# Reordering the first projections of an attention and GLU kernel, with half sums of the exponentials on GpSimd

## The chip, the cores and the metric

The kernel runs on one core of one Trainium2 chip. The metric is the time of one execution in device microseconds; the median of three runs of the kernel before is 205.53 us.

## The reference, cut to what matters

x has 2048 rows of 448; there are 16 heads of 28. `_layernorm` has no weights. The first block is an attention whose feature maps are softmaxes over the 28 elements of a head:

```python
h  = x  + _A_ref(_layernorm(x), wqkv, w_phi, wo)
h2 = h  + _B_ref(_layernorm(h), w_gate, w_up, w_down)

def _A_ref(x, wqkv, w_phi, wo):
    q, k, v = x @ wqkv, split into 16 heads of 28
    pq, pk = q @ w_phi, k @ w_phi                       # per head
    phi_q = concat(softmax(pq), softmax(-pq))
    phi_k = concat(softmax(pk), softmax(-pk))
    kv  = einsum("bhsf,bhsd->bhfd", phi_k, v);  z = sum over s of phi_k
    num = phi_q @ kv;  den = phi_q . z + 1e-6
    return (num / den) @ wo

def _B_ref(x, w_gate, w_up, w_down):
    return (sigmoid(x @ w_gate) * (x @ w_up)) @ w_down
```

## The kernel before

The 2048 rows are 16 tiles of 128. Products contract 64 rows at a time: two matmuls with 64 input rows each run side by side in the upper and lower half of the array, so a product over 448 inputs is written as two operations, an `a` with 8 matmuls and a `b` with 6; `b` adds to banks that `a` has just written with the other half of the array, and so waits until `a` has drained.

Every operation has a name, and every engine works off its names in an order that is written out by hand in the table `ORDER`, one string for each of `sp` (SyncE, which issues nearly all DMAs), `act` (ScalarE), `pe` (TensorE), `dve` (VectorE) and `pool` (GpSimd). A graph of reads and writes adds the semaphore waits; an operation may stand in the string of either of two engines (a copy out of PSUM on ScalarE or VectorE, for instance), and it runs on the engine in whose string its name stands. Nothing is reordered while the kernel runs: an operation that waits holds up all that follows on its engine.

The names that matter, with the number of a tile (0 to 15) behind most of them:

- `x0` to `x14`: loads of the input (x0 and x1 of one tile, the others of two). `ld_k`, `ld_v`, `ld_q`: the key, value and query weights; `ld_q` are four transposing DMAs into `WqT`. `ld_wo`, `ld_wg`, `ld_wu`, `ld_wd`: the weights of the output projection and of the GLU.
- `wT`, `wTe`: the key weights transposed on TensorE and copied out. `wsp`, `wex`: `w_phi` spread into a block diagonal matrix (with `hmask`). `w2m0_0` to `w2m0_3` and `w2e0_0` to `w2e0_3`: the key weights folded with `w_phi` into `Wk`, by a product and a cast out of PSUM; `w2m1` and `w2e1` the same for the query weights (`Wq`). `w2m1_k` reads all four `WqT`, and the four share two banks, so `w2m1_3` and `w2m1_2` need the casts of `w2m1_1` and `w2m1_0`.
- `bst`, `agg`: mean and variance of a tile (VectorE). `pow1`: the scale, to the power -1/2 (GpSimd), for tiles 0, 1, 2, 3 singly, for 4 and 5, 6 and 7, then for 8 to 11 and for 12 to 15 in one instruction; `nm1` the negated mean. `xn`: the normalized tile. `xT`: its transpose, for tiles 0 to 3 on TensorE (`xT0e` to `xT3e` copy it out), from tile 4 on by a transposing DMA on SyncE's queue (4 to 15).
- `ppa`, `ppb` (tiles 0 and 1, then 2 and 3): the projected keys, into banks 0 and 1. `vva`, `vvb`: the values of the same tiles, into banks 2 and 3. From tile 4 on `pva`, `pvb` make keys and values of one tile side by side. `v1`: the values copied out. `ek`: exp and exp of the negated keys (ScalarE, two instructions), in a ring of five buffers.
- `ss`: the sums of the exponentials over each head, a reduction of 896 elements of bf16 into 32 (VectorE, L675); `rs`: their reciprocals; `phi`: the exponentials times those (L685; VectorE or GpSimd); `kva`, `kvb`: the product with the values, summed over all tiles in banks 6 and 7; `seed`: the small constant there. `kvzA` to `kvzD`: the masked copies out of them.
- `pqa`, `pqb`, `eq`: projected queries of 512 rows and their exponentials. `qs`, `num`, `rsm`, `qq`, `b`, `c`, `rden`, `o`: numerator, denominator and quotient of a tile; `oT`: its transpose (tiles 0 and 1 on TensorE with `oT0e`, `oT1e`; later ones by DMA). `woa`, `wob`: the output projection of two tiles; `bs2`, `h`, `hn`, `hT`: the residual, its normalization and transpose. `ga`, `gb`, `sig`, `hh`, `dn`, `dp`, `dm`, `fin`, `out`: the GLU.
- `warm`: matmuls of zeros. `wwo`, `wgu`: no instruction, only waits of TensorE for the weights of the later stages.

Banks of PSUM are shared: the joint products of an even tile reuse banks 0 and 2, of an odd tile 1 and 3, so `pva` of a tile waits for the `ek` and `v1` of two tiles before. Of the order before, the part of TensorE up to tile 5:

```python
"... w2m0_3 xT1 xT0 warm7 warm8 warm9 xT3 ppa0 ppb0 xT2 vva0 seed vvb0 ppa2 ppb2 vva2 vvb2 kva0 "
"w2m1_1 w2m1_0 kvb0 pva4 kva1 pvb4 pva5 w2m1_3 w2m1_2 pvb5 ..."
```

Of the kernel before, what the change touches and what calls it, by code (L numbers as in the profile page):

```python
# [6 lines left out]
ALU = mybir.AluOpType  # L7
ACT = mybir.ActivationFunctionType
AX = mybir.AxisListType
# [9 lines left out]
class Graph:  # L19
# [90 lines left out]
    def emit(self, nc):  # L110
# [86 lines left out]
D = 448  # L197
H = 16
DH = 28
# [82 lines left out]
    ),  # L282
    "pool": (
# [44 lines left out]
def build(nc, A_x, A_wqkv, A_w_phi, A_wo, B_w_gate, B_w_up, B_w_down, out):  # L328
    S = A_x.shape[1]
    assert A_x.shape[0] == 1 and A_x.shape[2] == D and S == 2048  # L330
    NT = S // P
    NCH = S // 512
    x_t = A_x[0].rearrange("(p n) d -> p n d", p=P)
    out_t = out[0].rearrange("(p n) d -> p n d", p=P)
    wd_v = B_w_down.rearrange("(ft p) n -> p ft n", p=P)
    NV2 = 4
    NX, NO, NH, NPHI, NS, NE, NV, NSG, NHH = 3, 4, 3, 3, 4, 5, 5, 4, 2

    with ExitStack() as es:
        def sb(name, shape, d=dt.bfloat16):  # L340
            return es.enter_context(nc.sbuf_tensor(name, shape, d))
        f32 = dt.float32
        ident = sb("ident", [P, P])
# [676 lines left out]
```

## Time and profile before

| | us |
|---|---|
| median of three runs | 205.53 (205.25 to 205.82) |
| span of the profiled execution, first to last instruction | 202.0 |
| the two apart | 3.5 |
| TensorE busy | 196.1 |
| VectorE busy | 132.2 |
| ScalarE busy | 92.7 |
| GpSimd busy | 56.4 |

The page gives of the profiled execution its span alone, 202.0 us; the 3.5 us between it and the median of the runs lie before the first and after the last instruction. The granted clock of TensorE is 1.00 in every stretch named here. In the profile a row of the timeline is start, duration, engine, line, operation, what it writes and reads with sizes, and how many instructions were merged; the brackets at its end tell how long the engine had been idle and who ended that. PE is TensorE, PEld its loads of weights, DVE VectorE, ACT ScalarE, POOL GpSimd, SPq the queue of SyncE.

### The profile page before, as it was taken

To read this page: it belongs to the slowest core of one execution; us is meant where nothing else is said; L and a number is where in the kernel's file an instruction comes from. 1 tells how busy PE (TensorE), PEld (TensorE's weight loads), DVE (VectorE), ACT (ScalarE), POOL (GpSimd) and SP (SyncE) were. 2 spreads that over 40 slices of the span, in tenths; PEclk is the share of its full clock that TensorE was granted. 3 is DMA by queue.
4 is the path that set the end of the run, shared out by engine and by line. 5 is a ranking of instruction groups with operands and counts; after the bars stand their busy time and mean duration, and the time that the engine had idled before them with its cause. 6 is when DMAs were issued, how large, how long until landed. Compare 5 with 4: busy or idle time off the path is not lost.

```text
span 202.0 us, 5885 instructions
## 1 busy us (share of the span) xinstructions
PE 196.1 (97%) x2516; PEld 113.1 (56%) x2516; DVE 132.2 (65%) x319; ACT 92.7 (46%) x191; POOL 56.4 (28%) x95
## 2 busy tenths in 40 slices
PE   7899999999989999999999999999999999999995
PEld 4735656565558778676444444555555555554443
DVE  4899999978899677767758977436432422272224
ACT  3768998899772636222333342324422212222220
POOL 6579949533433613600041010001400000000000
PEclk9999999999999999999999999999999999999999
DMA  6955345849963320251005311030312000004003
GB/s 170 281 117 158 68 83 78 237 154 285 292 181 86 65 43 3 52 81 29 0 3 123 81 26 26 5 73 28 71 33 52 0 3 0 0 3 136 0 0 94
DMA packets 32491, 16.27 MB, mean 81 GB/s; under 512 B 24720, under 2 KB 31568, under 8 KB 32464
## 3 DMA queue, kind: packets, MB, share of 16 engines
q1 hardware_dynamic: 32336, 15.86, 32.0%
q8 instruction: 20, 0.33, 0.7%
q14 instruction: 7, 0.06, 0.1%
q10 hardware_dynamic: 128, 0.03, 0.1%
HBM read 8.34 MB, written 1.84 MB: 50 GB/s over the span
## 4 chain that ended last, share of the span: by engine, by line
PE 91%; DVE 4%; DMA 2%; SPq 1%; issue 1%; POOL 1%
PE psum L311 84%; PE psum L941 5%; DMA x_sb<-in_A_x_dram 2%; SPq L415 1%; DVE st L545 1%; PE psum L538 1%; DVE st L829 1%; POOL rst L833 1%; PE psum L612 0%; DVE hn_pad L851 0%; DVE xnT L531 0%; DVE b_sb L801 0%; DVE Wk L531 0%; DVE c_sb L804 0%; DVE rsm L798 0%
## 5 line engine op out<-in xcount | busy, mean ns | idle before, releaser
L311 PE MATMUL psum<-xnT,wg_sb 64*128 64x512 bf16 (+1 forms) x490 | 93.1, 333 | 0.2
L311 PE MATMUL psum<-xnT,wu_sb 64*128 64x512 bf16 (+1 forms) x490 | 92.9, 333 | 0.0
L913 ACT ACTIVATE sg_sb<-psum 128x512 bf16<-128x512 f32 (+1 forms) x70 | 34.8, 511 | 91.3 <-PE psum L311 90.8
L914 DVE SCALAR_TENSOR_TENSOR hhT<-sg_sb,psum 128x512 bf16<-128x512 bf16 (+1 forms) x70 | 38.9, 576 | 54.4 <-ACT sg_sb L913 54.2
L311 PEld LDWEIGHTS psum<-xnT,wg_sb 64*128 64x128 bf16 x490 | 44.4, 94 | 22.5 <-DVE hhT L914 4.2
L311 PEld LDWEIGHTS psum<-xnT,wu_sb 64*128 64x128 bf16 x490 | 44.4, 94 | 13.1
L311 PE MATMUL psum<-wd_sb,hhT 64*128 64x448 bf16 x336 | 36.9, 349 | 0.0
L311 PEld LDWEIGHTS psum<-wd_sb,hhT 64*128 64x128 bf16 x336 | 17.6, 94 | 14.5 <-DVE x_sb L836 0.5
L311 PE MATMUL psum<-Wk,xnT 64*128 64x448 bf16 x112 | 22.1, 350 | 0.2
L311 PE MATMUL psum<-wv_sb,xnT 64*128 64x448 bf16 x112 | 22.2, 351 | 0.1
L845 POOL TENSOR_SCALAR ve<-ssq 128x1 f32<-128x1 f32 x11 | 2.2, 200 | 55.0 <-ACT junk L842 54.8
L675 DVE TENSOR_REDUCE ss<-hhT 128x32 f32<-128x896 bf16 x16 | 16.6, 1054 | 0.3 <-ACT hhT L672 0.2
L721 ACT ACTIVATE eq<-psum 120x1024 bf16<-120x1024 f32 x16 | 15.7, 1024 | 1.0 <-PE psum L311 0.8
L685 POOL TENSOR_TENSOR phi<-hhT,rs 128x896 bf16<-128x896 bf16 x8 | 13.6, 1711 | 6.2 <-DVE rs L681 3.8
L311 PE MATMUL psum<-xnT,Wq 64*120 64x512 bf16 x112 | 15.0, 384 | 0.1
L810 POOL TENSOR_TENSOR o_pad<-c_sb,rden 128x448 bf16<-128x448 bf16 x10 | 9.3, 935 | 14.9 <-DVE rden L806 14.8
L311 PE MATMUL psum<-wo_o,oT 64*128 64x448 bf16 x56 | 13.2, 349 | 0.0
L311 PE MATMUL psum<-wo_e,oT 64*128 64x448 bf16 x56 | 13.1, 349 | 0.0
L941 PE MATMUL psum<-wd_sb,hhT 128*128 128x448 bf16 (+2 forms) x70 | 11.1, 315 | 0.0
L948 DVE SCALAR_TENSOR_TENSOR x_sb<-psum,x_sb 128x448 bf16<-128x448 f32 (+2 forms) x17 | 9.4, 592 | 2.7 <-PE psum L941 1.6
L311 PEld LDWEIGHTS psum<-Wk,xnT 64*128 64x128 bf16 x112 | 7.7, 94 | 5.6 <-PE psum L311 1.0
L801 DVE TENSOR_TENSOR b_sb<-psum,qq 128x464 bf16<-128x464 f32 x16 | 10.2, 637 | 0.7 <-PE psum L311 0.5
(103 smaller groups left out, 234.0 us busy)
## 6 DMA issues: line engine op xcount, KB each, us to landing
out_dram<-x_sb SPq DMA_DIRECT2D x15, 112.0 KB, 1.8
x_sb<-in_A_x_dram SPq DMA_DIRECT2D x7, 224.0 KB, 4.0
wd_sb<-in_B_w_down_dram SPq DMA_DIRECT2D x7, 224.0 KB, 4.0
wg_sb<-in_B_w_gate_dram SPq DMA_DIRECT2D x3, 448.0 KB, 6.3
wu_sb<-in_B_w_up_dram SPq DMA_DIRECT2D x3, 448.0 KB, 6.7
wv_sb<-in_A_wqkv_dram SPq DMA_DIRECT2D x2, 224.0 KB, 3.9
wk_sb<-in_A_wqkv_dram SPq DMA_DIRECT2D x2, 196.0 KB, 3.5
wo_e<-in_A_wo_dram SPq DMA_DIRECT2D x1, 336.0 KB, 3.1
```

The lines of the kernel that those rows point to most:

```text
L311: p = e.matmul(o, lhsT=w, rhs=r, start=st, stop=sp, tile_position=(row, 0))
L415: return op(eng, name, lambda e: e.dma_start(dst, src), r=r, w=w, dma="in" if eng == "sp" else "ain", nring=48 if eng == "sp" else 8, kb=kb)
L675: op("dve", "ss%d" % t, lambda e: e.tensor_reduce(ss[:, s, :].rearrange("p (b h) -> p b h", h=2), eks.rearrange("p b (d h) -> p b h d", h= ...
L685: return e.tensor_tensor(phi[:, sp, :, :, :].rearrange("p b a n -> p (b a) n")[:, :, 0:56].rearrange("p b (d h) -> p b d h", h=2), eks.rea ...
L721: op("act", "eq%d_%d%s" % (c, i, "pm"[sg]), lambda e, sg=sg: e.activation(eq[c][:, sg, 2 * i:2 * i + 2, :].rearrange("p g n -> p (g n)"), ...
L801: op("dve", "b%d" % t, lambda e: e.tensor_tensor(h3(b_sb), OMv[:, :, :, 0:EV], h2(qq)[:, :, :, None].to_broadcast([P, NB, 8, EV]), ALU.mul ...
L810: return e.tensor_tensor(o_pad[:, t % NO, off:off + D].rearrange("p (h d) -> p h d", h=H), c_sb[:, t % NS, :, 0:DH], rden[:, t % NS, :][:, ...
L845: op(("pool", "dve"), "ve%d" % t, lambda e: e.tensor_scalar(ve2[:, t:t + 1], ssq2[:, t:t + 1], 1.0 / D ** 3, EPS, op0=ALU.mult, op1=ALU.ad ...
L913: op("act", "sig" + nm, lambda e: e.activation(sg_sb[:, k, 0:N], bk(bg)[:, 0:N], ACT.Tanh, scale=0.5), r=[B(bg)], w=[("sg", k)])
L914: op("dve", "hh" + nm, lambda e: e.scalar_tensor_tensor(out=hhT[(t0 // 4) % NHH][:, ff, ns], in0=sg_sb[:, k, 0:N], scalar=1.0, in1=bk(bu)[ ...
L941: p = e.matmul(bk(b)[:, lo:hi], lhsT=hb[:, ff, TS(t)], rhs=wd_sb[:, ff, lo:hi], start=ff == 0, stop=ff == FT - 1)
L948: op("dve", "fin%d%s" % (t, nm), lambda e: e.scalar_tensor_tensor(out=h_sb[:, t, lo:hi], in0=bk(b)[:, lo:hi], scalar=0.5, in1=h_sb[:, t, l ...
```

## The change

It has three parts. The two loads of the value weights move in SyncE's queue from places 7 and 12 to places 6 and 7, right behind x2, and with that x4, x8 and x6 move back; `vva0` stands first of TensorE's products, ahead of `ppa0`. For six key tiles (3, 5, 7, 9, 11, 13) GpSimd adds the two halves of each group of 56 exponentials into a float32 buffer of 448 elements (`hs`, four buffers, in the space of `hhT0`, which the GLU uses later), and `ss` of such a tile reduces these. And the orders of all five engines are written anew up to the middle of the attention: the normalization of tile 0 stands ahead of the statistics of tiles 2 and 3; all four `w2m1` come before `pva4`; of the `phi`, four run on GpSimd instead of eight; `kvzA` goes to VectorE and `kvzD` to ScalarE; `o1` to VectorE, `oT1e` to ScalarE; `rden6` stands behind `h3` and `h2`, and `nm2` ahead of `o6`; `wwo` and `wgu` stand later; two `warm` are gone. From `ga0_10` on the order of TensorE is as it was.

```diff
     "sp": (
-        "x1 x0 ld_k0 ld_k2 x2 x4 ld_v2 x8 x6 ld_q2 ld_q1 ld_v0 x10 ld_q0 ld_q3 xT4 x12 x14 xT5 xT6 xT7 xT8 xT9 xT10 "
+        "x1 x0 ld_k0 ld_k2 x2 ld_v2 ld_v0 x4 x8 x6 ld_q2 ld_q1 x10 ld_q0 ld_q3 xT4 x12 x14 xT5 xT6 xT7 xT8 xT9 xT10 "
...
     "act": (
-        "wphi kvzones nm1_1 wTe0 wTe2 wTe3 w2e0_0 nm1_3 w2e0_2 w2e0_1 xT0e xT3e ek0 ek1 v1_0 nm1_6 v1_1 ek3 ek2 v1_2 "
-        "v1_3 w2e1_1 nm1_8 w2e1_0 ek4 v1_4 w2e1_2 ek5 v1_5 w2e1_3 v1_6 ek6 nm1_12 v1_7 ek7 ek8 v1_8 eq0_0p ek9 v1_9 "
...
+        "wphi wTe0 wTe2 wTe3 w2e0_2 w2e0_0 w2e0_3 nm1_3 nm1_4 ek0 ek1 v1_1 v1_0 w2e1_1 ek2 w2e1_0 v1_2 ek3 v1_3 "
+        "w2e1_2 ek4 v1_4 nm1_8 ek5 v1_5 w2e1_3 v1_6 ek6 par ek7 v1_7 ek8 v1_8 ek9 v1_9 ek10 kvzones v1_10 ek11 v1_11 "
...
     "pe": (
-        "warm0 warm1 warm2 wsp warm3 wT0 wT1 warm4 wT2 wT3 warm5 w2m0_0 w2m0_1 w2m0_2 warm6 w2m0_3 xT1 xT0 warm7 "
-        "warm8 warm9 xT3 ppa0 ppb0 xT2 vva0 seed vvb0 ppa2 ppb2 vva2 vvb2 kva0 w2m1_1 w2m1_0 kvb0 pva4 kva1 pvb4 pva5 "
-        "w2m1_3 w2m1_2 pvb5 pva6 kvb1 kva2 pvb6 kvb2 pva7 pqa0_0 pvb7 pva8 kva3 pvb8 kvb3 pqb0_0 pva9 kva4 pvb9 pva10 "
...
+        "warm0 warm1 warm2 warm3 wsp warm4 wT1 wT0 xT0 wT2 wT3 warm5 warm6 w2m0_2 w2m0_0 xT1 w2m0_1 w2m0_3 warm7 vva0 "
+        "ppa0 ppb0 xT3 xT2 vvb0 ppa2 w2m1_1 ppb2 vva2 w2m1_0 vvb2 w2m1_3 w2m1_2 seed pva4 kva0 pvb4 pva5 kvb0 kva1 "
+        "pvb5 pva6 kvb1 kva2 pvb6 pva7 pqa0_0 pvb7 pva8 kvb2 pvb8 kva3 pva9 kvb3 kva4 pvb9 kvb4 kva5 pva10 kvb5 pvb10 "
...
     "dve": (
-        "zero hmask mask2 bst1 bst0 agg1 agg0 wex wTe1 bst3 bst2 agg3 xn0 agg2 bst4 xT1e w2e0_3 agg4 bst5 xn2 agg5 "
-        "bst7 bst9 bst6 xT2e agg6 agg7 ss0 bst11 rs0 ss1 bst10 bst8 rs1 agg10 agg8 agg9 agg11 par phi1 bst12 ss2 "
...
+        "zero bst1 bst0 agg0 agg1 hmask mask2 xn0 wex wTe1 xT0e bst2 bst3 agg2 agg3 xT1e w2e0_1 bst5 bst4 agg5 agg4 "
+        "bst6 xn2 bst7 agg6 xT3e agg7 xT2e ss0 bst10 rs0 ss1 bst9 bst11 rs1 bst8 bst13 ss2 agg8 agg10 agg9 bst15 "
+        "agg11 rs2 bst14 phi2 agg13 bst12 ss3 agg12 ss4 agg15 rs3 agg14 ss5 rs4 ss6 rs5 rs6 xn11 phi4 phi5 xn12 ss8 "
...
     "pool": (
-        "phipad opad0 neghalf ident0 ident zsel steps epsl0 v1ones pow1_1 pow1_0 xn1 pow1_3 xn3 pow1_2 nm1_4 pow1_4 "
-        "epsr0 xn4 pow1_6 xn5 phi0 xn6 wqpad xn7 pow1_8 xn8 phi2 xn9 xn10 phi4 pow1_12 xn13 phi7 xn15 phi8 phi9 phi10 "
-        "phi13 o0 o1 o2 o3 pow2_0 pow2_1 o4 o5 o6 o7 nm2 ve2 pow2_2 hn2 ve3 nm3 pow2_3 hn3 nm7 ve4 pow2_5 pow2_4 "
...
+        "steps neghalf epsr0 zsel ident0 v1ones epsl0 opad0 phipad ident wqpad pow1_0 nm1_1 pow1_1 xn1 pow1_3 pow1_2 "
+        "xn3 pow1_4 xn4 xn5 pow1_6 nm1_6 xn6 phi0 xn7 phi1 hs3 pow1_8 xn8 xn9 hs5 xn10 phi3 pow1_12 nm1_12 hs7 xn13 "
+        "hs9 hs11 xn15 hs13 phi13 o0 o2 o3 pow2_0 pow2_1 o4 o5 nm2 o6 o7 ve2 pow2_2 hn2 ve3 nm3 pow2_3 hn3 nm7 ve4 "
...
+        hs = hhT[0][:].rearrange("p f n -> p (f n)").bitcast(f32)[:, 0:NHS * D].rearrange("p (s b x) -> p s b x", s=NHS, x=DH)
...
             eks = ek[:, s, :, :, :].rearrange("p b a n -> p (b a) n")
-            op("dve", "ss%d" % t, lambda e: e.tensor_reduce(ss[:, s, :].rearrange("p (b h) -> p b h", h=2),
-                                                            eks.rearrange("p b (d h) -> p b h d", h=2), AX.X, ALU.add),
-               r=[("ek", s)], w=[("ss", s)])
+            if "hs%d" % t in g.where:
+                sh = t % NHS
+                op("pool", "hs%d" % t, lambda e: e.tensor_tensor(hs[:, sh], eks[:, :, 0:DH], eks[:, :, DH:2 * DH], ALU.add),
+                   r=[("ek", s)], w=[("hs", sh)])
+                src, key = hs[:, sh].rearrange("p b (d h) -> p b h d", h=2), ("hs", sh)
+            else:
+                src, key = eks.rearrange("p b (d h) -> p b h d", h=2), ("ek", s)
+            op("dve", "ss%d" % t, lambda e: e.tensor_reduce(ss[:, s, :].rearrange("p (b h) -> p b h", h=2), src, AX.X, ALU.add),
+               r=[key], w=[("ss", s)])
```

More of the change, by code (lines that the diff above doesn't have):

```diff
@@ L336, in build @@
     NV2 = 4
-    NX, NO, NH, NPHI, NS, NE, NV, NSG, NHH = 3, 4, 3, 3, 4, 5, 5, 4, 2
+    NX, NO, NH, NPHI, NS, NE, NV, NSG, NHH, NHS = 3, 4, 3, 3, 4, 5, 5, 4, 2, 4
     with ExitStack() as es:
@@ L526, in warm @@
             return f
-        for i, (n, size) in enumerate(((4, 512), (2, 512), (1, 128), (2, 128), (1, 128), (6, 128), (4, 128), (6, 128), (8, 128), (2, 128))):
+        for i, (n, size) in enumerate(((4, 512), (2, 512), (1, 128), (2, 128), (1, 128), (6, 128), (4, 128), (6, 128))):
             op("pe", "warm%d" % i, warm(n, size), r=["zero"], w=[B(3)])
```

63 rows, old and new, of the table ORDER are left out of this document.

## The prediction, made before the changed kernel ran

> **What bounds the kernel now.** The page comes first, for the busy shares and the chain by engine; then the busy time of one stretch; then the start of the chain in order of time.
>
> ```profile
> PE 196.1 (97%) x2516; PEld 113.1 (56%) x2516; DVE 132.2 (65%) x319; ACT 92.7 (46%) x191; POOL 56.4 (28%) x95
> ```
> ```profile
> 18.00:43.50 25.50, 25.48 (x434) 15.45 (x434) 24.70 (x47) 22.77 (x51) 18.18 (x15) 1.00 0.53 122
> ```
> ```profile
> 2.60 4.05 DMA x_sb<-in_A_x_dram
> ...
> 6.68 1.15 DVE st L545 x2
> ```
>
> TensorE is busy 97% of the span, so a gain can only be an earlier start of its work or a gap that closes; the change removes no product. From 18.00 to 43.50 TensorE is busy 25.48 of 25.50 us, but VectorE (third pair of numbers, 24.70) and ScalarE (fourth, 22.77) hardly less: three engines run at the same pace, and TensorE can move forward only as far as the two others follow. Ahead of that the chain is the load of x2 (in at 6.65) and, on VectorE, the statistics of tiles 2 and 3 and what is queued behind them, up to the first product at 10.11.
>
> **The start: to the first key product (ppa0).** Rows of the timeline, in order of time:
>
> ```profile
> 4.21 1.08 POOL L554 TENSOR_TENSOR rst<-mv,neghalf 128x1 f32<-128x1 f32 x2 [0.84 <-DVE mv L546]
> 4.95 0.62 DVE L494 TENSOR_TENSOR Wphi<-psum,hmask 112x448 bf16<-112x448 f32 x1 [0.69 <-PE psum L490]
> 5.72 0.39 DVE L531 COPY WkT<-psum 112x448 bf16<-112x448 bf16 x1 [0.15 <-PE psum L599]
> 7.84 0.37 DVE L573 TENSOR_SCALAR xn_pad<-x_sb,mv,rst 128x512 bf16<-128x512 bf16 x1
> 8.07 1.18 ACT L531 CAST Wk<-psum 128x448 bf16<-128x448 f32 x2
> 8.73 0.41 DVE L531 COPY xnT<-psum 128x512 bf16<-128x512 bf16 x1
> 9.06 0.65 DVE L531 CAST Wk<-psum 128x448 bf16<-128x448 f32 x1
> 10.11 1.74 PE L311 MATMUL psum<-Wk,xnT 64*128 64x448 bf16 x14
> ```
>
> The normalization of tile 0 (xn0, 7.84) had its scale at 5.29 (4.21 + 1.08), but stood behind the statistics of tiles 2 and 3 in VectorE's queue. After the change it stands ahead of them, behind hmask and mask2, and its scale is the first of the two: xn0 4.9 to 5.25, wex to 5.85, wTe1 to 6.25, the copy of tile 0's transpose (xT0e, 0.41) to 6.65; the load of x2 keeps its place in SyncE's queue, so the statistics still begin at 6.68 and take 1.15, two aggregates and xT1e (0.41) follow to 8.45, and w2e0_1 0.65 to 9.1. The other three Wk casts stand on ScalarE; two of them took 1.18 and ended at 9.25, with a small nm1_3 in between that now follows: also about 9.1. The value product vva0 needs only xT1e: 8.5. Its eight matmuls hold TensorE 0.75 (eight in 0.93 below, less the last one's tail), so ppa0 starts at 9.2 instead of 10.11: **0.9 earlier**.
>
> ```profile
> 3.58 0.43 SPq L415 DMA_DIRECT2D wv_sb<-in_A_wqkv_dram  x1
> ```
> ```profile
> DMA to landing us min/median/max: 3.5/3.9/4.3
> ```
>
> That holds if wv is in. Its second half is now issued seventh, at about 3.6, the slot of the row above, and landed 3.5 to 4.3 after issue in the two loads of before (answer for the tile wv_sb): 7.1 to 7.9, under 8.45. x4, x8 and x6 move back by one or two slots of 0.45 and as many transfers; their statistics stand behind w2e0_1 (9.1), so this costs nothing; without that cover VectorE would wait for the rest of their landing.
>
> **From ppa0 to the first joint product (pva4).**
>
> ```profile
> 11.89 0.54 ACT L671 ACTIVATE hhT<-psum 128x448 bf16<-128x448 f32 x1 [1.09 <-PE psum L311]
> 12.11 0.93 PE L311 MATMUL psum<-wv_sb,xnT 64*128 64x448 bf16 x8
> 13.18 0.56 ACT L672 ACTIVATE hhT<-psum 128x448 bf16<-128x448 f32 x1
> 13.80 1.74 PE L311 MATMUL psum<-Wk,xnT 64*128 64x448 bf16 x14
> 17.14 0.57 PE L612 MATMUL psum<-Wphi,WqT 112*128 112x112 bf16 x8
> 17.29 1.01 ACT L531 CAST v<-psum 128x448 bf16<-128x448 f32 x2
> 18.00 0.35 PE L311 MATMUL psum<-Wk,xnT 64*128 64x448 bf16 x1
> ```
> ```profile
> 9.89 1.26 SPq L503 DMA_TRANSPOSE WqT<-in_A_wqkv_dram  x1
> ```
> ```profile
> DMA to landing us min/median/max: 3.8/4.3/4.9
> DMA to landing us min/median/max: 4.1/4.1/4.1
> ```
>
> ppa2 overwrites the banks that ek0 and ek1 read, so it waits for ScalarE: ek0 began at 11.89, right after ppb0, ek1 ended at 13.74, ppa2 began at 13.80. After: ppb0 ends 9.2 + 1.74 = 10.95, ek1 12.85, ppa2 12.9. TensorE now idles some 1.0 there, since the value product that had filled the gap went ahead: making it first buys nothing beyond the 0.9. Next comes a new wait: w2m1_1, now right behind ppa2 (before: after kva0, at 17.14), needs all four WqT transposes. They landed 3.8 to 4.9 after issue (first line: all four; second: the last alone). The last was issued at 9.89 and landed at 13.99; after the change as many transfers stand before it in SyncE's queue, so I take 14.0 again (13.7 to 14.8 by the bounds), 0.3 after ppa2's 13.65. Behind it in TensorE's queue are ppb2, vva2, vvb2, and ek2 waits for ppb2. ScalarE then runs w2e1_1 from 14.4 (as many elements as a Wk cast; 0.65), ek2 (two of 0.54 to 0.56, overlapped: 1.0), w2e1_0 (0.65) and v1_2 (half of 1.01), with small overlaps: 17.1, and pva4, which reuses v1_2's bank, starts at 17.1 against 18.00: **still 0.9 earlier**. By then all four w2m1 are done, of which two (half of 0.57) came later before, while the short kva0 and kvb0 are not, and the w2m1 fill the drains between the two halves of a product pair: **0.2 more**, 1.1 at pva8.
>
> **The middle: half sums on GpSimd, and the transposes.**
>
> ```profile
> L675 DVE TENSOR_REDUCE ss<-hhT 128x32 f32<-128x896 bf16 x16 | 16.6, 1054 | 0.3 <-ACT hhT L672 0.2
> L685 POOL TENSOR_TENSOR phi<-hhT,rs 128x896 bf16<-128x896 bf16 x8 | 13.6, 1711 | 6.2 <-DVE rs L681 3.8 <-PE psum L311 2.4
> L685 DVE TENSOR_TENSOR phi<-hhT,rs 128x896 bf16<-128x896 bf16 x8 | 4.6, 592 | 0.0
> ```
> ```profile
> L810 POOL TENSOR_TENSOR o_pad<-c_sb,rden 128x448 bf16<-128x448 bf16 x10 | 9.3, 935 | 14.9 <-DVE rden L806 14.8
> ```
> ```profile
> 16.52 0.77 POOL L576 TENSOR_SCALAR xn_pad<-x_sb,nm,rst 128x512 bf16<-128x512 bf16 x1
> 16.94 0.34 DVE L546 BATCH_NORM_AGGREGATE mv<-st 128x2 f32<-128x9 f32 x4
> 17.42 1.06 POOL L576 TENSOR_SCALAR xn_pad<-x_sb,nm,rst 128x512 bf16<-128x512 bf16 x1
> 18.45 1.01 POOL L554 TENSOR_TENSOR rst<-mv,neghalf 128x4 f32<-128x4 f32 x1
> 20.42 1.50 SPq L583 DMA_TRANSPOSE xnT<-xn_pad  x1
> 25.46 0.35 PE L311 MATMUL psum<-wv_sb,xnT 64*128 64x448 bf16 x1
> 27.81 0.35 PE L311 MATMUL psum<-Wk,xnT 64*128 64x448 bf16 x1
> ```
> ```profile
> DMA to landing us min/median/max: 2.4/2.6/4.0
> ```
>
> A whole sum of 896 elements takes 1.054; half the elements take between 0.53 and that (no row has float32 input); I take 0.60, near the lower end, since the statistics of 448 elements take no more (1.15 for two). Six tiles save VectorE 2.7. Four more phi go to VectorE (12 instead of 8): 4 x 0.59 = 2.4. GpSimd loses 4 x 1.71 = 6.8 and gains six hs. No row is an add into float32; nearest is the product of 448 elements, 0.935, the upper bound is the whole 896, 1.71; I take 0.95, 5.7 in all. So the exchange is nearly even on both, and pays by itself nothing: the tiles that end the stage, 14 and 15, keep whole sums.
>
> What the new order does move is the statistics of tiles 8 to 11, which share one scale instruction (pow1_8) on GpSimd. VectorE works without a gap from 6.68 in both orders. Before, agg11 was the last of the four aggregates that end at 17.28. After, there stand in addition before it two statistics (0.58 each), one sum (1.05) and one transpose copy (0.41), and xn0 (0.37) has gone ahead: 2.25, or 2.0 with the overlaps, so agg11 ends near 19.4. Then pow1_8 1.01, some 0.15, xn8 0.77: xT8 is issued at 21.4 to 21.6, not 20.42, and lands 2.6 later, about 24.1. The first wv product of pva8 started at 25.46, so it comes at 24.35: just in time. xT9, issued 1.5 behind it, lands 2.4 to 4.0 later, mostly near 2.6 to 3.1: about 26.2. pva9 was at 27.81; earlier by 1.1 and by pqb0_0 (0.7), which is now put behind it, it comes at 26.0. **Loss 0.25** (0 if xT9 takes 2.6, 1.0 at 4.0).
>
> One row speaks against the change: xn7 took 1.06 where its like took 0.77, while VectorE ran a phi beside it (17.23 to 17.84). [...] At 0.3 for each of the four added phi on VectorE, GpSimd loses up to 1.2, and one such hit before xT8 makes the gain 0.3 less. [...]
>
> **After the middle.**
>
> ```profile
> 65.30 0.56 DVE L836 SCALAR_TENSOR_TENSOR x_sb<-psum,x_sb 128x448 bf16<-128x448 f32 x1
> 66.42 1.19 SPq L823 DMA_TRANSPOSE oT<-o_pad  x1
> 70.62 0.35 PE L311 MATMUL psum<-wo_e,oT 64*128 64x448 bf16 x1
> ```
>
> o1 goes to VectorE, oT1e and one kvz part to ScalarE; both have spare time before num6, whose wait (the c5 of VectorE) stays as it was: nothing. But rden6 is put behind the residuals h2 and h3, which end at 65.86 now and at 65.1 then; o6 on GpSimd takes 0.94 behind it, so oT6 is issued near 66.3 and oT7, 1.19 behind it, near 67.5 instead of 66.42. With 2.4 to 2.6 for landing that is 70.0, where woa6 (70.62) would come at 69.8: **loss 0.15** (0 to 0.4). From gate and up on, the order is the old one.
>
> **Sum.** -0.9 - 0.2 + 0.25 + 0.15 = -0.7. The profiled span of 202.0 becomes 201.3; the median of the three runs, 205.53, holds 3.5 around it, unchanged: **204.8**.
>
> **Rivals.** (1) Slower: GpSimd becomes the bound. hs3 stands before pow1_8, hs5 before xn10, hs7 before xn13. At 0.95 hs3, behind ek3, ends at 19.4, about when agg11 does; at 1.71, or with collisions, each pushes its follower by up to 0.75, two of them xn10 and phi3 by 1.5, and TensorE, which by this working meets tiles 8 to 10 just in time, waits 1 to 1.7. The gain is gone from 1.4 us per hs; at 1.7 the time is 206.2. For it: by this working GpSimd has hardly a gap from 14 to 28. Against: the 0.935 row. Chance 0.28. (2) No change: the last WqT transpose takes 4.9 and lands at 14.8, which holds TensorE at w2m1_1 and ScalarE at ek2 0.8 longer, or xT9 takes 4.0, which costs 0.75 more than I took; either leaves next to nothing, 205.5. For it: all of these times stand in the rows. Against: each is the slowest of its row. Chance 0.28. (3) The forecast, with its better side: without any wait for the x transposes and for oT7 the 1.1 stays whole, 204.4. Chance 0.44.
>
> **Numbers.** 0.3% is 0.6 us, about what a measurement of this kernel can tell from no change. Likeliest: 204.8, its own range 204.3 to 205.1; over all cases 204.0 to 206.4. Faster by over 0.3% 0.44, within 0.28, slower 0.28.
>
> **What would show it.** In the profile after: the first product a wv product at 8.5; ppa0 at 9.2; a TensorE gap near 1.0 before ppa2 at 12.9; a short wait for WqT; pva4 at 17.1; sums of 0.60 and hs of 0.95; xT8 issued near 21.5; the last kv product 0.7 to 0.9 before 44.1. Wrong it is if ppa0 comes after 9.6, hs takes over 1.4, or TensorE's waits for xnT between 24 and 30 add up to over 1.

## The result: slower, and the profile after

Six timed runs each: the changed kernel has a median of 207.66 us (205.76 to 208.18), the kernel before 205.36 (203.68 to 205.82) beside it; the ratio is 1.0124 (95% interval 1.0084 to 1.0164). The forecast of 204.8, with a range up to 206.4, was wrong. The ratios and intervals leave out single runs over 1.5% above their kernel's fastest (one each of e_ot, e_front and e_wide below, which the medians include) and are not quotients of medians. The profiled execution has a span of 205.3 and its own time was 207.04: a run is its span and some 1.8 more (204.59 around 202.7 and 204.97 around 203.2 in two later ones). The 202.0 that the forecast started from is thus an execution of about 203.8, one of the quickest of before, not one of its median.

Names as above; the line numbers of the changed kernel are larger by one at the start and by up to eight further on. First the page of the changed kernel, its busy times:

```profile
PE 197.5 (96%) x2506; PEld 115.3 (56%) x2506; DVE 132.5 (65%) x323; ACT 92.4 (45%) x190; POOL 54.8 (27%) x98
```

TensorE is busy 1.4 us longer than before with ten matmuls fewer. Where, its own rows of the timeline at the start tell:

```profile
4.03 1.63 PE L491 MATMUL psum<-wph,zsel 112*112 112x28 bf16 x16
5.86 0.99 PE L600 MATMUL psum<-ident,wk_sb 112*112 112x112 bf16 x8
7.82 1.27 PE L525 MATMUL psum<-zero 128*128 128x128 bf16 x10
10.48 0.50 PE L525 MATMUL psum<-zero 128*128 128x128 bf16 x6
10.92 0.93 PE L311 MATMUL psum<-wv_sb,xnT 64*128 64x448 bf16 x8
11.68 0.54 PE L311 MATMUL psum<-Wk,xnT 64*128 64x448 bf16 x4
```

Eight 112-column matmuls take 0.99 here and 0.62 in the profile of before; from start to start it is 0.093 against 0.052, and 0.107 against 0.055 for 128 columns. At 10.1 the spacing halves: up to there TensorE ran at half speed, in the profile of before only up to 4.1. The page's clock row does not show this: this page has none, and that of before reads full from its first slice on. It is read from the rows. So the value product came at 10.92 instead of 8.5 and ppa0 at 11.68 instead of 9.2.

Further on, the pieces of the chain of waits where TensorE did not run on:

```profile
13.45 0.54 ACT hhT L672
14.00 0.43 ACT hhT L673
14.43 0.44 ACT hhT L672
14.87 0.45 ACT hhT L673
...
49.42 0.59 issue
...
71.20 1.70 PE psum L311 x28
72.91 1.02 issue
```

The first four are ek0 and ek1, for which ppa2 waits (a gap of 0.7 on TensorE). "issue" is a wait that the profile does not name. The one at 49.42, in the middle of num2, is in none of the other profiles. The one at 72.91 is woa6; VectorE and GpSimd show what it waits for:

```profile
67.91 0.36 DVE L813 RECIPROCAL rden<-c_sb 128x16 f32<-128x16 bf16 x2
68.28 1.83 POOL L817 TENSOR_TENSOR o_pad<-c_sb,rden 128x448 bf16<-128x448 bf16 x2
69.24 2.50 SPq L830 DMA_TRANSPOSE oT<-o_pad  x2
73.92 0.35 PE L311 MATMUL psum<-wo_e,oT 64*128 64x448 bf16 x1 [1.02 <-issue]
```

rden6 and rden7 run together at 67.91, o6 and o7 behind them, oT6 and oT7 behind those (the latter issued at 70.48), and woa6 starts as oT7 lands at 73.83.

The groups by shape, for the half sums:

```profile
L683 DVE TENSOR_REDUCE ss<-hhT 128x32 f32<-128x896 bf16 x10 | 10.5, 1058 | 0.1
L692 DVE TENSOR_TENSOR phi<-hhT,rs 128x896 bf16<-128x896 bf16 x12 | 7.1, 611 | 0.0
L678 POOL TENSOR_TENSOR hhT<-hhT 128x448 f32<-128x448 bf16 x6 | 6.2, 1030 | 4.6 <-ACT hhT L673 4.6
L683 DVE TENSOR_REDUCE ss<-hhT 128x32 f32<-128x448 f32 x6 | 3.7, 613 | 0.3 <-POOL hhT L678 0.3
```

A sum of half a tile takes 0.613, an hs 1.03 in the mean (median 0.970; the longest, 1.22, ran beside a phi of VectorE). And the stretch from pva4 to the end of the kv product, on TensorE, VectorE, ScalarE and GpSimd (second, fourth, fifth and sixth number), first after, then before:

```profile
19.72:45.39 25.67, 25.52 (x459) 15.22 (x459) 24.41 (x54) 23.62 (x51) 16.64 (x17) 1.00 0.45 97
```
```profile
18.00:44.11 26.11, 25.90 (x450) 15.77 (x451) 24.70 (x47) 23.38 (x51) 18.18 (x15) 1.00 0.52 120
```

It is 0.44 shorter. Start by start, after less before: ppa0 +1.57, pva4 +1.72, kvb15 +1.28, num2 +1.32, woa0 +1.88 (the stall at 49.42), num7 +2.07, woa6 +3.31, the end +3.28. So the start and woa6 make the loss, not the half sums.

### The profile page after: what moved, and what is told of

It is laid out like the page before. It is cut to its first block, busy times and chain, and to the rows that moved or that the text cites. A ratio compares the mean times of both kernels' runs of the same rounds, so it can differ in the third digit from the quotient of the medians.

```text
span 205.3 us, 5870 instructions
## 1 busy us (share of the span) xinstructions
PE 197.5 (96%) x2506; PEld 115.3 (56%) x2506; DVE 132.5 (65%) x323; ACT 92.4 (45%) x190; POOL 54.8 (27%) x98
## 4 chain that ended last, share of the span: by engine, by line
PE 89%; ACT 3%; DVE 2%; DMA 2%; issue 1%; SPq 0%; DVEq 0%
PE psum L311 80%; PE psum L948 5%; DMA wk_sb<-in_A_wqkv_dram 2%; ACT eq L728 1%; PE psum L613 1%; PE psum L600 1%; PE psum L525 1%; PE psum L539 1%; ACT kvz L761 1%; DVE st L836 1%; ACT hhT L672 0%; ACT x_sb L837 0%; ACT hhT L673 0%; SPq L416 0%; DVE hn_pad L858 0%
## 5 line engine op out<-in xcount | busy, mean ns | idle before, releaser
L683 DVE TENSOR_REDUCE ss<-hhT 128x32 f32<-128x896 bf16 (+1 forms) x16 | 14.0, 891 | 0.4 <-POOL hhT L678 0.3
L817 POOL TENSOR_TENSOR o_pad<-c_sb,rden 128x448 bf16<-128x448 bf16 x9 | 8.3, 935 | 13.9 <-DVE rden L813 13.9
L546 DVE BATCH_NORM_STATS2 st<-x_sb 128x6 f32<-128x448 bf16 x16 | 9.2, 604 | 2.0 <-DMA x_sb<-in_A_x_dram 2.0
```

The lines of the kernel that those rows point to most:

```text
L546: op("dve", "bst%d" % t, lambda e: e.bn_stats(st1[:, t, 0:6], x_sb[:, t, :]), r=[("x", t)], w=[("st1", t)])
L683: op("dve", "ss%d" % t, lambda e: e.tensor_reduce(ss[:, s, :].rearrange("p (b h) -> p b h", h=2), src, AX.X, ALU.add), r=[key], w=[("ss", s)])
L817: return e.tensor_tensor(o_pad[:, t % NO, off:off + D].rearrange("p (h d) -> p h d", h=H), c_sb[:, t % NS, :, 0:DH], rden[:, t % NS, :][:, ...
```

## The experiments

All profiles together first, since the first reading needs them. "Full speed" is where the spacing of TensorE's matmuls halves. Each ratio is to runs of before on the same chip, whose medians lie between 205.1 and 205.4.

| kernel | full speed at | ppa0 | span | timed median (lowest to highest), runs | ratio to before (95%) |
|---|---|---|---|---|---|
| before | 4.1 | 10.11 | 202.0 | 205.36 (203.68 to 205.82), 6 | |
| b_again | 8.9 | 11.33 | 203.2 | 204.97, 1 | |
| after | 10.1 | 11.68 | 205.3 | 207.66 (205.76 to 208.18), 6 | 1.0124 (1.0084 to 1.0164) |
| a_again | 3.9 | 9.41 | 202.7 | 204.59, 1 | |
| b_rden6 | 4.3 | 9.83 | 202.5 | 204.39, 1 | |
| e_ot | 9.0 | 11.00 | 204.4 | 205.40 (203.46 to 207.51), 12 | 1.001 (0.9971 to 1.0048) |
| e_nohs | 10.4 | 11.61 | 205.8 | 207.32 (206.16 to 208.92), 6 | 1.0113 (1.0065 to 1.0162) |
| e_front | 10.0 | 11.46 | 204.3 | 205.98 (204.12 to 207.80), 12 | 1.0043 (1.0014 to 1.0072) |
| b_wide | 5.7 | 10.40 | 202.3 | 204.06 (203.35 to 204.47), 12 | 0.9957 (0.9931 to 0.9983) |
| a_wide | 4.0 | 9.52 | 203.0 | 205.94 (204.58 to 206.80), 12 | 1.0034 (1.0004 to 1.0064) |
| e_wide | 7.2 | 10.31 | 204.1 | 204.19 (203.38 to 207.63), 12 | 0.9978 (0.9945 to 1.0011) |
| b_lean | 4.1 | 10.07 | 201.9 | 203.93 (203.60 to 204.54), 12 | 0.9944 (0.9920 to 0.9968) |
| e_lean | 6.5 | 9.97 | 201.8 | 203.60 (202.93 to 205.58), 12 | 0.9949 (0.9916 to 0.9983) |
| e_lean_b | 7.1 | 10.26 | 203.5 | 204.72 (203.13 to 206.06), 12 | 0.9996 (0.9960 to 1.0032) |
| e_lean2 | 4.5 | 9.71 | 203.3 | 205.02 (203.81 to 205.29), 12 | 0.9995 (0.9966 to 1.0024) |
| f_lean | 4.9 | 9.67 | 204.9 | 204.83 (204.06 to 206.67), 12 | 1.0004 (0.9971 to 1.0037) |

### Both kernels once more: b_again and a_again

No edit. Theory A has the point of full speed differ between executions of one kernel; theory B has the order of the first microseconds decide it.

> The kernel before, once more, for a second profiled execution. In its first one 128-column matmuls followed each other every 0.055 to 0.06 us from 4.1 us on. [...] Theory B (the order of the first microseconds decides): full speed at about 4.1 again, span 202.0 within 0.3.

> The changed kernel once more. Its first profile had 128-column matmuls 0.11 us apart up to 10.0 us. Theory A: the point of full speed lies elsewhere, and if it lies near 4 to 7 us ppa0 comes 1 to 2 us before 11.68 and the span shrinks from 205.3 by as much. Theory B: 10.0 again, span 205.3 within 0.3. Both: a gap near 1.0 before woa6, and the stall of 0.6 in num2.

Rows of the start, first of the second execution of before, then of the changed kernel's:

```profile
3.81 1.63 PE L490 MATMUL psum<-wph,zsel 112*112 112x28 bf16 x16
5.46 0.95 PE L599 MATMUL psum<-ident,wk_sb 112*112 112x112 bf16 x8
11.33 0.93 PE L311 MATMUL psum<-Wk,xnT 64*128 64x448 bf16 x8
```
```profile
3.95 0.96 PE L491 MATMUL psum<-wph,zsel 112*112 112x28 bf16 x16
5.18 0.62 PE L600 MATMUL psum<-ident,wk_sb 112*112 112x112 bf16 x8 [0.20 <-DMA wk_sb<-in_A_wqkv_dram]
9.41 0.75 PE L311 MATMUL psum<-Wk,xnT 64*128 64x448 bf16 x6
```

The two have changed places: now before's wsp takes 1.63 and its ppa0 comes 1.22 later than in its first profile, and every later start by the same 1.22; the changed kernel's takes 0.96 and its ppa0 comes 2.27 earlier. The gap before woa6 is there again (1.10), the stall in num2, which both theories expected, is not. Theory A holds: the point of full speed belongs to the execution, not to the order (4.1 and 8.9 in before, 10.1 and 3.9 in the changed kernel). In 29 timed runs of before that stood beside e_wide and b_wide, nine lay between 203.5 and 204.0, twenty between 204.9 and 205.9 and none between; of all 121 timed runs of before, four lie between 204.1 and 204.8.

At like speed the change can be read: a_again less the first profile of before is -0.69 at ppa0, -0.51 at pva4, -0.94 at kvb15, -0.66 at num7, and +0.65 at woa6 and to the end.

### The order of rden6: e_ot and b_rden6

e_ot, in the changed kernel's order of VectorE (and nm2 on GpSimd behind o6 and o7):

```diff
-hh0_1 hh0_0 rsm7 qq7 b7 c7 hh0_2 hh0_3 rsm8 h3 h2 rden6 rden7 qq8
+hh0_1 hh0_0 rden6 rsm7 qq7 b7 c7 hh0_2 hh0_3 rsm8 h3 h2 rden7 qq8
```

> The changed kernel with rden6 moved back in VectorE's order to its old place behind hh0_0 (ahead of rsm7), and nm2 on GpSimd behind o6 and o7. If the wait of 1.02 before woa6 comes from rden6 standing behind rsm8 (which waits for num8), the gap goes and the kernel is 1.0 to 1.2 us faster than the changed one, ratio to the kernel before near 1.006. If something else (the transposes' own landing of 3.35) holds woa6, the time stays within 0.3 of the changed kernel, ratio 1.012.

b_rden6, in the order of before (and nm2 ahead of o6):

```diff
-hh0_0 rden6 rsm7 qq7 b7 c7 hh0_2 hh0_3 h2 rden7 h3 rsm8 qq8
+hh0_0 rsm7 qq7 b7 c7 hh0_2 hh0_3 rsm8 h3 h2 rden6 rden7 qq8
```

> The kernel before with only the tail of that stretch of VectorE's order as the change has it: rsm8 h3 h2 rden6 rden7 instead of rden6 ahead of rsm7, and nm2 ahead of o6 on GpSimd. If the wait before woa6 is made by this order alone, the distance from num8 to woa6 grows from 6.43 us (6.42 in the second profile of before) to 7.5 to 7.8, as in the two profiles of the changed kernel (7.66, 7.74). If it needs the rest of the change, 6.4 to 6.7.

From num8 to woa6 it is 6.43 in before, 7.66 and 7.74 in after and a_again, 6.47 in e_ot: the order makes the wait, and putting rden6 and nm2 back takes 1.2 out of it. The ratio fell from 1.0124 to 1.001 where 1.006 was expected: the median is 2.3 lower, and 1.1 of that does not come from this wait.

But b_rden6 has 6.82, near neither forecast: the order alone costs 0.39. GpSimd's rows show a part that the prediction had not priced, nm2 in front of o6 and o7 (b_rden6):

```profile
66.16 0.24 POOL L839 TENSOR_SCALAR nm<-sum 128x1 f32<-128x1 f32 x1 [4.65 <-DVE x_sb L835]
66.37 1.83 POOL L809 TENSOR_TENSOR o_pad<-c_sb,rden 128x448 bf16<-128x448 bf16 x2
```

That holds o6 and o7 up by 0.2. rsm8 in front of h3, which e_ot's expectation names as the cause, costs 0.05: h2 and h3 end 1.72 after the start of num8 here and 1.67 after it in before.

The rest is in the landing. The DMAs from oT7's issue to its landing, in after and in b_rden6 (the packets by queue, then each issue with its time to landing):

```profile
q14 instruction: 1, 0.01, 1.3%
issues: line engine op xcount, KB each, median us to landing
oT<-o_pad SPq DMA_TRANSPOSE x1, 3.4
```
```profile
q1 hardware_dynamic: 1073, 0.26, 51.1%
issues: line engine op xcount, KB each, median us to landing
oT<-o_pad SPq DMA_TRANSPOSE x1, 2.5
```

Where a packet of an instruction queue went between, 1.9 us after the issue, the transpose took 0.9 longer; so in after, a_again, a_wide and e_nohs (3.35 to 3.43), and not in b_rden6. In e_ot such a packet comes 3.2 after the issue, and oT7 lands after 2.42. So 0.4 of order and 0.85 of landing, for the changed order issues oT7 1.9 before such a packet. That the packet does it is so far a coincidence, taken up below.

### Without the half sums: e_nohs and e_front

e_nohs takes hs3 to hs13 out of GpSimd's order, so VectorE sums all tiles whole; e_front is e_ot without half sums and with three of the phi that the change moved put back on GpSimd:

```diff
-xn9 hs5 xn10 phi3 pow1_12 nm1_12 hs7 xn13 hs9 hs11 xn15 hs13 phi13
+xn9 xn10 phi3 pow1_12 nm1_12 xn13 phi6 xn15 phi8 phi10 phi13
```

> The changed kernel without the six half sums: VectorE sums all 16 tiles whole, GpSimd does nothing in their place. If the half sums pay for the four phi that went to VectorE, VectorE has 2.7 us more to do between 18 and 43 and num0 comes 1 to 2 us later: ratio to before 1.017 to 1.022. If the half sums are what slows the changed kernel (GpSimd the bound, theory 1 of the prediction), it is faster by 1 or more: ratio 1.005 or less.

> e_ot without half sums, with phi6, phi8 and phi10 back on GpSimd: the new start and little else. If the exchange of half sums against phi pays by itself nothing, as the prediction has it, the stage from pva4 to kvb15 is within 0.4 of e_ot's and the time within 0.5 of e_ot. If the half sums are what makes the stage keep up, it is 1 or more slower than e_ot, as e_nohs was in its profile.

The stretch from pva4 to the end of the kv product, in e_nohs and then in a_again:

```profile
19.65:46.48 26.83, 26.01 (x460) 15.50 (x460) 26.30 (x54) 24.07 (x51) 10.56 (x11) 1.00 0.46 111
```
```profile
17.49:43.17 25.68, 25.53 (x460) 15.18 (x460) 24.44 (x55) 23.62 (x51) 16.68 (x17) 1.00 0.46 106
```

Without half sums VectorE is busy 26.30 of 26.83: it is the bound, and the stage is 1.15 longer; with three phi given back (e_front, 19.49 to 46.14) still 26.65. TensorE then waits for VectorE's phi at kva9, 0.57 in e_nohs. So the half sums are worth about 1.0 here, and GpSimd, busy 16.68 of 25.68, is no bound: rival 1 is out. e_ot's own stage, with which e_front was to be compared, is 27.15, longer than e_front's by a late transpose of tile 8 (below); hence the comparison with a_again.

The timed runs do not settle it, and neither expectation names what came. e_front is 0.58 over e_ot (0.5 or less, or 1 or more, were expected), with intervals that overlap; e_nohs lies level with after (1.0113 and 1.0124), between the two ranges given.

### What opens TensorE's clock: e_wide, b_wide and a_wide

```diff
-p = e.matmul(bk(2)[:GP, gg * DH:(gg + 1) * DH], lhsT=..., rhs=wph[:, m * DH:(m + 1) * DH], ...)
+p = e.matmul(bk(2)[:GP, gg * DH:gg * DH + GP].rearrange("p (c f) -> p c f", f=DH), lhsT=...,
+             rhs=wph[:, None, m * DH:(m + 1) * DH].to_broadcast([GP, 4, DH]), ...)
```

e_wide has this on top of e_ot, b_wide on top of before, a_wide on top of the changed kernel. Theory C has the wide matmuls bring full speed early in every execution: for e_wide by 7 us, with a median near 204 and a spread of 2 or less. Theory D has the width make no difference.

> e_ot with the 16 small matmuls of wsp made four times as wide (112 columns, their 28 repeated), which at half clock take the same 0.092 us each. [...] Theory D: the width does not matter, the openings lie at about 4 or at 9 to 10 as before: median 205.4 within 0.6, spread unchanged.

> The kernel before with the same wide wsp. Theory C: all runs near the early ones of before, 203.6 to 204.4, ratio 0.994 to 0.997. Theory D: ratio 1.000 within 0.002.

> The changed kernel, its order untouched, with the wide wsp of e_wide and b_wide, so that both sides can be compared with TensorE at full speed by 7 us. By the profiles at like clock (a_again 202.7 against 202.0) the change by itself costs about 0.7, and 1 more where full speed comes at 7 instead of 4: median 204.6 to 205.6, that is 0.5 to 1.5 above b_wide's 204.06. If what remains of the loss at full clock is larger (2 as in the first comparison), 206 or more; if the clock was the whole loss, 204.1 or less. The distance from num8 to woa6 stays at 7.3 to 7.8.

Rows of b_wide, to be held against b_again's above: sixteen wide matmuls in 1.70, and full speed soon after them.

```profile
3.81 1.70 PE L490 MATMUL psum<-wph,zsel 112*112 112x112 bf16 x16
5.52 0.65 PE L599 MATMUL psum<-ident,wk_sb 112*112 112x112 bf16 x8
```

The width matters. Of eight profiles with the narrow wsp three had full speed at 3.9 to 4.3 and five at 8.9 to 10.4; all eight with the wide one (these three and the five below) had it between 4.0 and 7.2, six of them between 4.5 and 7.2, where no narrow one has it. b_wide's twelve runs lie within 1.1 us, near before's early ones, and it is faster than before, as theory C has it: 0.9957 (0.9931 to 0.9983). e_wide's median came out as that theory expected (204.19), its spread did not: 203.4 to 207.6, over 4 where 2 or less was expected. So in the new order the clock is not all that scatters. The five late executions (8.9 to 10.4) were at half speed 7.7 to 9.2 us after the first matmul at 1.2, b_again with hardly a pause of TensorE. At half speed the sixteen wide matmuls take no longer than the narrow ones: 1.50 in e_wide (4.03 to the next operation's start at 5.53), 1.47 in after (4.03 to 5.50). What sets the point, why it moves from one execution to the next and how the width acts on it, no run shows.

For the changed kernel itself (a_wide) this is no cure. Its distance from num8 to woa6 is 7.68, as expected; its profile is 0.7 longer than b_wide's (203.0 and 202.3), as expected; but its median, 205.94, is 1.9 over b_wide's and outside the 204.6 to 205.6 given. Five runs lie at 204.6 to 205.1, seven at 205.9 to 206.8. The profiled run is one of the five; the two groups lie about 1.3 apart, the price of a late transpose of tile 8 (below), but no trace of the seven shows that it was this.

### Fewer warming matmuls, and the scatter: e_lean, b_lean, f_lean, e_lean2, e_lean_b

The lean kernels drop the ten matmuls of warm5 and warm6: e_lean from e_wide, b_lean from b_wide, f_lean from e_front with the wide wsp. e_lean2 drops the six of warm7 too. e_lean_b is e_lean.

> e_wide without the ten warming matmuls warm5 and warm6, which only keep TensorE busy while it has the work of the start to do. If TensorE at half clock is what holds ppa0 in late executions, ppa0 comes 0.5 to 1.0 earlier than in e_wide's profile (10.31) and the median falls from 204.19 to 203.3 to 203.8, faster than before and than b_wide. If the ten matmuls are needed for the clock, full speed comes at 9 to 10 and the median rises to 205 or more. Twenty instructions less also put TensorE's instruction packets about 0.55 later against its work: the transpose of tile 15, hit by one in e_wide (4.40 to land), is then missed and lands in 2.5, and another one is hit.

> b_wide without the ten warming matmuls warm5 and warm6. In before ppa0 waits for the casts of the key weights and not for TensorE, and its first x transposes stand behind them anyway; so at full clock nothing, at most 0.3: median 203.7 to 204.2. If e_lean's gain comes from the ten matmuls alone, 203.6 or less, and nothing of it is due to the change.

> e_lean without half sums, with phi6, phi8 and phi10 back on GpSimd: the new start, the wide wsp, the ten matmuls less, the old order of rden6. If the exchange of half sums against phi pays nothing, within 0.3 of e_lean (203.6). If it pays 0.7 to 1.0, as pva4 to kvb15 of e_front (26.65) against a_again and e_lean (25.68) suggests, 204.2 to 204.7.

> e_lean also without the six matmuls of warm7 in front of vva0. vva0 may start when xT1e ends, 0.2 earlier, ppa0 is held by the casts of the key weights and gains 0.1 at most. Twelve instructions less put TensorE's packets some 0.2 to 0.3 later against its work, so the one behind the transpose of tile 15 (2.25 after its issue in e_lean) moves out of reach: if packets make the scatter, at most one of twelve runs lies over 204.5 and the median is 203.3 to 203.6; if not, two to four lie there as in e_lean.

> e_lean once more: median 203.6 within 0.3, two to four of twelve runs over 204.5; in the profile the transpose of tile 15 lands in 2.5 when the packet starts 2.25 or more behind its issue and in over 4 when it starts 1.0 to 2.2 behind it.

e_lean's median was as expected, 203.60, but its ppa0 came 0.34 before e_wide's instead of 0.5 to 1.0, and its full speed came 0.7 sooner too. e_lean_b, the same kernel on another chip, has 204.72, with eight of twelve runs over 204.5 where two to four were expected; its full speed at 7.1 is nearly e_wide's, and its ppa0 only 0.05 earlier. So the ten matmuls themselves were worth next to nothing. b_lean is level with b_wide (203.93 and 204.06), as expected. e_lean2 missed: 205.02 instead of 203.3 to 203.6, and nine of twelve runs over 204.5, more than either case given. f_lean's 204.83 is a little over the 204.2 to 204.7 for half sums that pay, and in its profile kva9 waits 1.78 for VectorE's phi; but e_lean_b, with half sums, is level with it. So e_lean is no settled gain over b_lean; the kernels that beat both before and after with a narrow spread are b_wide and b_lean, which hold the old order.

The scatter lies in the transposes. That of tile 15, its DMAs up to 2.2 us after its issue, in e_lean and then in e_wide:

```profile
xnT<-xn_pad SPq DMA_TRANSPOSE x1, 2.5
```
```profile
q8 instruction: 1, 0.02, 3.5%
issues: line engine op xcount, KB each, median us to landing
...
xnT<-xn_pad SPq DMA_TRANSPOSE x1, 4.4
```

A packet of 16 KB of queue q8, instructions, starts 1.97 after the issue in e_wide and 2.25 after it in e_lean: 4.40 against 2.47 to landing, and pva15 waits 1.59 in e_wide. That it would be missed was expected of e_lean before it ran, though by a shift of 0.55 and not of 0.28; e_lean_b, as expected, had 2.27 and 2.48. The 144 transposes of tiles 7 to 15 in all sixteen profiles, by the packet of instructions that started from 0.5 before to 2.6 after their issue (q8 before q14 where there were both):

| packet | started after the issue, us | transposes | landed after, us |
|---|---|---|---|
| q8, 16 KB | -0.40 to 0.81 | 30 | 2.45 to 3.49 |
| q8 | 0.98 to 1.34 | 7 | 3.35 to 4.44 |
| q8 | 1.80 to 2.06 | 19 | 3.95 to 4.52 |
| q8 | 2.20 to 2.31 | 12 | eleven 2.41 to 2.48, one 4.22 |
| q8 | 2.54 and 2.57 | 2 | 4.55 and 2.74 |
| q14, 8 KB | 1.19 to 2.07 | 22 | 3.08 to 3.63 |
| q14 | 0.26 to 0.61 and 2.18 to 2.40 | 10 | 2.40 to 2.51 |
| none | | 42 | 2.41 to 2.61 |

The lesser delay of the smaller packets is the one seen at oT7. It holds further on: fourteen oT and hT with a packet of q8 1.81 to 2.08 after their issue landed after 4.03 to 4.36, and of 131 hT without a packet none took over 2.51. Not every late landing has a packet beside it: oT2 to oT4, among the loads of the weights, take up to 5.91 without one. The packets of q8 come every 5 to 13 us up to 80. Before and after have 20 of them each, to 2516 and 2506 matmuls and as many loads of weights on TensorE: one to 126 matmuls in the mean, 62 to 181 between two. That they are TensorE's, and so come later against its work where it has fewer instructions, is inferred from these counts; with twenty instructions less the packet at tile 15 came 0.28 later in e_lean and 0.30 later in e_lean_b than in e_wide.

In the new order tile 8 matters most, since pva8 needs it as soon as it lands. e_ot's longest wait of TensorE behind the start:

```profile
PE psum L310 <- DMA xnT<-xn_pad: 1.3, 1, 1.3
```

xT8 was hit (a packet of q8 1.95 to 2.05 after its issue) in e_ot, f_lean, e_lean2 and e_lean_b (4.00 to 4.24), and from pva7 to pva8 it is 3.44 to 3.67 there; in the other seven profiles of the new order the packet came 0.13 before to 0.49 after the issue, and it is 2.18 to 2.46. A hit costs 1.25 to 1.5. In b_lean xT8 was hit too (4.52), and pva8 lost nothing: the old order leaves it slack. e_lean2's expectation looked at tile 15, which was missed as said (2.47), while tile 8 took the hit; that tile 8 is the one that counts was seen only afterwards, and no run was made to move its packet. What puts q8's packet before xT8 in one execution and 2 us behind it in the next is open.

## Why the prediction was wrong

- **"The median of the three runs holds 3.5 us around it, unchanged"** failed. Of the 3.5, only 1.8 lie around a span; the rest is what most executions of before lose to a later full speed, and the profiled one did not. Every duration of TensorE at the start was read from that one profile, with full speed at 4.1.
- **ppa0 at 9.2, 0.9 earlier.** At early full speed 9.41, 0.69 earlier: vva0 at 8.66 and the casts hold as described: the mechanism was right, the size 0.2 too large. At late full speed TensorE itself is the bound up to ppa0 (5.86 to 11.68 without a gap), which the prediction had as waiting for casts: 11.00 in e_ot against 11.33 in b_again, only 0.33 earlier at nearly the same opening (9.0 and 8.9), and 11.68 where it came at 10.1. This step of the prediction fails there.
- **From ppa0 to pva8** held: the gap before ppa2 is 0.7 (forecast 1.0); w2m1_1 did not wait in after and a_again, the last WqT being in at 13.3 and 13.9 (in e_lean2, with 14.6, it waited 0.45); pva4 lost 0.2 against ppa0, and 0.35 more was won up to pva8 (forecast 0.2).
- **Half sums** held in size: 0.613 (0.60) and 0.97 (0.95). "Pays by itself nothing" was wrong to the good: about 1.0 in the profiles, since without it VectorE is the bound.
- **The transposes of the middle.** xT8 was issued at 21.77 in a_again (forecast 21.4 to 21.6) and landed just in time, and kvb15 came 0.94 earlier (0.85). That the sum is so near is in part luck: pva8 was only 0.86 earlier, not 1.1, and xT9, landing after 2.52, cost nothing where 0.25 was taken. The step that failed: "lands 2.6 later" for xT8, where its row's 4.0 was only tried on xT9. Four of eleven profiles of the new order pay 1.25 to 1.5 there, though after and a_again do not.
- **rden6, "loss 0.15"** was mis-sized eightfold: 1.25, and 0.2 at ga0_1 where nothing was forecast, its cause not looked into. This is the term that turns the sum. The prediction priced rden6 behind h2 and h3; it left out nm2, which now stands ahead of o6 (0.2), and rsm8 ahead of h3 (0.05): with them the order costs 0.39. The other 0.85 is oT7's landing, 3.35 instead of 2.5, beyond the "2.4 to 2.6" taken.
- **Rival 1** (GpSimd the bound) had the sign by another cause: no hs is over 1.4 (the longest, 1.22 beside a phi of VectorE, is 0.25 over the median), and where TensorE waits between 24 and 30 (e_ot), it is for DMA. **Rival 2** had the right mechanism, a transpose of 4.0, on the neighbour of the one that counts.

Summed at early full speed: -0.94 at kvb15, +0.28 at ga0_1 and before it, +1.31 at woa6, +0.65 in all where -0.7 was forecast. At late full speed, after less b_again: +0.35 at ppa0, back to +0.07 at kvb15, +0.60 from the stall at 49.42, +1.2 at woa6, 2.1 in all with the small ones. That is near the 2.3 of the timed medians, but it is one execution of each, and the stall, unexplained and in no other profile, is part of it. How often a timed run has an xT8 hit beside its late full speed can't be told without its trace.

## What to carry to other kernels

One profile is one execution: before a time is built on its rows, see at which speed its first matmuls run and set the sum on the time of that same run. When an operation is moved in a hand-written order, price everything that now stands ahead of it, on every engine of its chain up to the landing, small operations too. And a transfer that is forecast to land "just in time" is priced with the slow end of its row, for a reordering that uses up its slack pays that end in some executions.

## What the runs showed of the hardware

- TensorE's half speed lasts to about 4 us or to 9 to 10 us here, by execution; with sixteen small matmuls made four times as wide, in 1.50 instead of 1.47, none of eight profiles has the late case (4.0 to 7.2): 205.1 to 204.06 for the kernel before, more than the 0.7 forecast for the change.
- A packet of 16 KB of instructions that starts 1.8 to 2.06 us after a DMA transpose's issue goes with a landing of 3.95 to 4.52 instead of about 2.5 (19 of 19); one of 8 KB at like distance with 3.08 to 3.63; without either, 42 transposes took 2.41 to 2.61. It was not caused on purpose; e_lean against e_wide is the one case where missing it was said ahead.
